# An attention-plus-mixture kernel on one core: TensorE's order chosen while the program is emitted, relu on the freer engine, the first batch loaded in three pieces

## The chip, the cores and the metric

The kernel runs on one core of one Trainium2 chip. The metric is the device time of one execution in microseconds (us), as the median of several runs. All runs told here are of the state that is listed as fast. TensorE's clock is not always granted in full: every record of it in these profiles says either full or half rate (in the kernel before, half at 40.6 to 47.5 us and at 64.5 to 71.4 us, full between them).

The profile names engines in short: PE is TensorE (matrix products), PEld its weight loads, DVE VectorE, ACT ScalarE, POOL GpSimd, SP SyncE. L365 is line 365 of that kernel.

## The reference

```python
# q, k, v: (4 batches, 8 heads, 768 positions, 64);  n_sink = 4, window = 128
scores = q @ k.T / sqrt(64)
keep   = (key < 4) | (0 <= query - key < 128)        # "sink" keys, and a sliding window
x      = softmax(where(keep, scores, -1e9)) @ v      # -> (3072 tokens, 512)
p      = domain_probs / (domain_probs.sum(-1) + 1e-9)  # (3072, 4)
out    = sum over 4 experts e of  p[:, e] * (relu(x @ w1[e]) @ w2[e])   # w1: 512x1024, w2: 1024x512
```

Attention is little work and has long chains (product, exp, mask, product, division, transpose). The mixture is much work and has short ones (product, relu; product, scaled addition). Attention of batch b+1 is therefore mixed into the mixture of batch b. Batch 0 has no earlier mixture to hide in.

## The kernel before

TensorE runs its products in the order of the program, so the order in which the kernel emits them decides what waits for what. The kernel before emits by a fixed pattern. Attention units (batch, head pair, group of 256 queries) go through three product steps with a lag of one unit:

```python
def lagged(units):
    n = len(units)
    for i in range(n + 2):
        if i < n:
            scores(*units[i]); yield          # then exp on ScalarE, mask on VectorE
        if i >= 2:
            turn(*units[i - 2])               # transpose of the scaled values
        if 1 <= i <= n:
            values(*units[i - 1])             # then 1/sum and scaling on VectorE
        yield
```

The mixture pays out attention steps by a counter of TensorE time. In batch 0 there is one step per 500 ns, and later one per 2200 ns. A first-layer part can't start before all attention of its tokens is emitted:

```python
def spent(ns):
    clock["pe"] += ns
    while side and clock["pe"] >= clock["due"]:
        clock["due"] += clock["pace"]
        if next(side[0], "end") == "end": side.pop(0)

def mixture(b, e, part):
    t0, n = PARTS[b][part]                    # batch 0: 3 parts of 256 tokens; later: 2 of 384
    while any((b, hp, t // G) not in turned for ...):
        next(side[0])                         # attention first, whatever it waits for
    for fb in range(NFB):                     # 8 blocks of the hidden layer
        ... 4 matmuls into hp_ (two PSUM banks in turn)
        nc.scalar.activation(out=ht, in_=hp_, func=AF.Relu)
        spent(4 * (n / 2.4 + 3))
        if fb % 2 == 1 and pending:
            pending.pop(0)()                  # second layer: 8 matmuls of 512 columns, DVE adds
    ...
```

The loads, in order of issue (sizes as read, 4 bytes an element): first 256 positions of q and k of batch 0 (1 MB); two blocks of v; w1 of expert 0 (2 MB); w2 of expert 0 (2 MB); the other 512 positions of q and k (2 MB); four blocks of v; w1 and w2 of experts 1 to 3 (12 MB); then q, k and v of batch 1.

The softmax here doesn't subtract the row's maximum and nothing guards it: scores larger than these inputs give would overflow.

## Time and profile before

| | before |
|---|---|
| median time | 447.5 us |
| span of the profile | 445.9 us |
| TensorE busy | 402.4 us |
| ScalarE, VectorE busy | 195.5, 156.3 us |
| end of the last product | 441.8 us |

The page of the kernel before, its parts 1 and 2. Part 2 cuts the span in 40 slices; a digit is the busy share in tenths, and in the row of the clock the granted share.

```profile
PE 402.4 (90%) x2858; PEld 228.5 (51%) x2900; DVE 156.3 (35%) x321; ACT 195.5 (44%) x361; POOL 45.6 (10%) x98
...
PE   2566758999999989999999989999999999999996
...
PEclk9998887999999999999999999999999999999999
DMA  9999996690000115900000110000000110000012
```

TensorE bounds the kernel from about 80 us on. In the first seven slices it is far from full, and DMA is full in the first six of them. A busy TensorE isn't a TensorE at its peak (from 40 to 60 us it is busy for 16.4 us and does 12.9 us of work by the count that follows), so I also counted work. To each product I gave its start-to-start time at full clock, from stretches where nothing waits: 216 ns for 512 columns, 162 for 384, 109 for 256, 56 for a transpose, 31 to 83 for the small attention products. The whole program is 380 us of such work. The rest is lost time. (This trace lacks some products: it has 726 of the 768 of the second layer. I scaled its sum to 380.)

The busy time of each engine in five stretches of the kernel before. The columns are stretch and length, then PE, PEld, DVE, ACT and POOL with numbers of instructions, granted clock, DMA share and GB/s.

```profile
0.00:20.00 20.00, 9.30 (x76) 5.79 (x76) 11.30 (x37) 7.03 (x11) 16.44 (x46) 1.00 1.17 193
20.00:40.00 20.00, 10.64 (x109) 7.52 (x109) 8.45 (x15) 10.58 (x15) 7.29 (x9) 1.00 1.44 199
40.00:60.00 20.00, 16.39 (x156) 10.62 (x158) 9.76 (x26) 8.15 (x15) 3.49 (x4) 0.83 1.21 208
60.00:80.00 20.00, 13.22 (x103) 8.95 (x103) 4.08 (x5) 6.89 (x12) 1.09 (x6) 0.83 0.94 89
80.00:340.00 260.00, 251.50 (x1893) 143.15 (x1921) 99.47 (x208) 126.55 (x236) 17.28 (x34) 1.00 0.22 31
```

The granted clock of 1.00 in the first two rows isn't a reading. The first record of the clock is at 30.4 us, and up to there consecutive transposes start 107 ns apart, against 56 ns from 30.9 us on: half rate.

By the count of work, the four stretches up to 80 us hold 34.9 us of the 380. From there to the last product the rate is 345.1 us of work in 361.8 us, or 95.4%.

What TensorE waited for in the kernel before (total us, times, longest us):

```profile
PE tr L218 <- DVE qo L100: 11.3, 3, 6.6
PE tx L303 <- DVE onat L294: 6.7, 11, 1.2
PE tr L218 <- ACT ko L98: 4.4, 2, 3.3
PE hps L390 <- ACT ht L396: 4.3, 9, 1.0
PE tr L218 <- DVE ko L100: 3.5, 1, 3.5
```

The transposes `tr` wait for q and k that have only just landed: at 22.0 and 24.6 us for the second piece of batch 0, and at 62.1 and 66.1 us for batch 1. The turn `tx` waits for VectorE's scaling, the first layer `hps` for relu.

### The profile page before, as it was taken

The page shows a single profiled execution, that of the slowest core. Times are in us where ns is not written, and L with a number is a line of the kernel's source. Part 1 is how long each engine was busy: PE and PEld are TensorE (multiplying, and loading weights), DVE is VectorE, ACT ScalarE, POOL GpSimd, SP SyncE. Part 2 cuts the span into 40 slices and gives each one's busy share as a digit, 9 for nine tenths or more (in the row PEclk, how much of TensorE's full clock was granted, in tenths as well). Part 3 has the DMA queues.
Part 4 walks back from the last instruction along what each step waited for, and adds up shares of the span by engine and source line. Part 5 has one row for each costly group of instructions (what it writes and reads, how often), then busy time and mean ns, then how long its engine had stood idle before and what let it go on. Part 6 is the DMA issues. An engine that isn't in the chain of part 4 may idle for free.

```text
span 445.9 us, 7024 instructions
## 1 busy us (share of the span) xinstructions
PE 402.4 (90%) x2858; PEld 228.5 (51%) x2900; DVE 156.3 (35%) x321; ACT 195.5 (44%) x361; POOL 45.6 (10%) x98
## 2 busy tenths in 40 slices
PE   2566758999999989999999989999999999999996
PEld 1344436656666655555555554555545555555552
DVE  3825521243444511444443412354442222222222
ACT  3256325545444465544443364454543333333330
POOL 9642100600000006000000010000000000000000
PEclk9998887999999999999999999999999999999999
DMA  9999996690000115900000110000000110000012
GB/s 185 203 193 209 210 195 43 84 129 1 1 2 24 72 49 79 134 2 1 1 1 0 72 71 1 1 1 1 0 1 1 71 72 1 0 1 0 1 47 94
DMA packets 45315, 25.16 MB, mean 56 GB/s; under 512 B 25804, under 2 KB 40140, under 8 KB 45284
## 3 DMA queue, kind: packets, MB, share of 16 engines
q0 software_dynamic: 39552, 17.30, 30.7%
q1 hardware_dynamic: 5732, 7.42, 4.7%
q8 instruction: 22, 0.36, 0.3%
q14 instruction: 9, 0.07, 0.1%
HBM read 35.73 MB, written 6.29 MB: 94 GB/s over the span
## 4 chain that ended last, share of the span: by engine, by line
PE 78%; DMA 12%; ACT 4%; issue 2%; POOL 2%; DVE 1%; ACTq 0%
PE mop L365 36%; PE hps L390 34%; DMA kn<-in_k_dram 8%; DMA vx_72<-in_v_dram 4%; PE sps L250 2%; PE tr L218 2%; ACT ht L396 2%; PE od L287 2%; ACT aT L260 1%; ACT qkT L221 1%; PE tx L303 1%; DVE out_sb L373 1%; PE od L281 1%; POOL vx_72 L109 0%; POOL qn L86 0%
## 5 line engine op out<-in xcount | busy, mean ns | idle before, releaser
L396 ACT ACTIVATE ht<-hps 128x384 bf16<-128x384 f32 (+1 forms) x288 | 128.9, 455 | 171.1 <-PE hps L390 169.2
L365 PEld LDWEIGHTS <-ht 128*128 128x128 bf16 x768 | 74.3, 98 | 79.4 <-issue 3.3
L373 DVE SCALAR_TENSOR_TENSOR out_sb<-mop,scale_t,out_sb 128x512 f32<-128x512 f32 x72 | 54.1, 751 | 140.4 <-PE mop L365 140.4
L260 ACT ACTIVATE aT<-sps 128x1024 bf16<-128x1024 f32 (+1 forms) x46 | 44.0, 957 | 33.8 <-PE sps L250 33.1
L390 PE MATMUL hps<-xT,w_0_88 128*128 128x384 bf16 (+1 forms) x288 | 52.6, 324 | 2.6 <-ACT ht L396 2.4
L390 PE MATMUL hps<-xT,w_2_305 128*128 128x384 bf16 (+1 forms) x288 | 48.8, 308 | 1.0 <-ACT ht L396 0.4
L390 PE MATMUL hps<-xT,w_3_309 128*128 128x384 bf16 (+1 forms) x288 | 48.4, 308 | 1.1 <-ACT ht L396 1.0
L390 PE MATMUL hps<-xT,w_1_301 128*128 128x384 bf16 (+1 forms) x288 | 48.8, 308 | 0.7 <-ACT ht L396 0.5
L365 PE MATMUL mop<-w_0_100,ht 128*128 128x512 bf16 x180 | 45.0, 385 | 0.8 <-issue 0.2
L365 PE MATMUL mop<-w_1_303,ht 128*128 128x512 bf16 x181 | 44.0, 379 | 0.7 <-issue 0.2
L365 PE MATMUL mop<-w_2_307,ht 128*128 128x512 bf16 x181 | 44.0, 379 | 0.7 <-issue 0.2
L365 PE MATMUL mop<-w_3_311,ht 128*128 128x512 bf16 x184 | 44.1, 379 | 0.4
L371 DVE TENSOR_SCALAR out_sb<-mop,scale_t 128x512 f32<-128x512 f32 x24 | 18.0, 751 | 59.5 <-PE mop L365 57.8
L390 PEld LDWEIGHTS <-w_0_88 128*128 128x128 bf16 x288 | 28.1, 103 | 20.1 <-issue 6.9
L261 DVE TENSOR_TENSOR aT<-aT,mask_93 128x1024 bf16<-128x1024 bf16 x32 | 22.1, 692 | 40.7 <-ACT aT L260 40.7
L390 PEld LDWEIGHTS <-w_3_309 128*128 128x128 bf16 x288 | 27.1, 98 | 17.7 <-issue 3.7
L390 PEld LDWEIGHTS <-w_1_301 128*128 128x128 bf16 x288 | 26.6, 97 | 17.0 <-issue 4.3
L390 PEld LDWEIGHTS <-w_2_305 128*128 128x128 bf16 x288 | 26.4, 97 | 16.7 <-issue 4.5
L221 ACT COPY qkT<-tr 128x1536 bf16<-128x1536 bf16 (+2 forms) x16 | 20.5, 1278 | 23.4 <-PE tr L218 23.4
L218 PE MATMUL tr<-ident,qo 128*128 128x128 bf16 x96 | 9.9, 238 | 13.2 <-DVE qo L100 11.3
L294 DVE TENSOR_TENSOR onat<-od,R 128x256 bf16<-128x256 f32 x48 | 20.4, 425 | 1.7
L303 PE MATMUL tx<-ident,onat 128*128 128x128 bf16 x96 | 14.0, 230 | 6.8 <-DVE onat L294 6.7
(73 smaller groups left out, 226.5 us busy)
## 6 DMA issues: line engine op xcount, KB each, us to landing
out_dram<-out_sb SPq DMA_DIRECT2D x24, 256.0 KB
qn<-in_q_dram POOLq DMA_DIRECT2D x3, 768.0 KB, 8.0
kn<-in_k_dram POOLq DMA_DIRECT2D x3, 768.0 KB, 10.9
vx_72<-in_v_dram POOLq DMA_DIRECT2D x12, 128.0 KB, 10.9
vx_73<-in_v_dram POOLq DMA_DIRECT2D x12, 128.0 KB, 12.1
w_0_88<-in_moe_w_dram POOLq DMA_DIRECT2D x1, 1024.0 KB, 10.3
w_0_100<-in_moe_w_dram POOLq DMA_DIRECT2D x1, 1024.0 KB, 14.2
w_1_301<-in_moe_w_dram POOLq DMA_DIRECT2D x1, 1024.0 KB, 16.1
```

Source lines behind the costliest of these rows:

```text
L218: nc.tensor.transpose(tr[:, i, t], nat[b, piece, name][:, t, 2 * hp:2 * hp + 2, :], ident,)
L221: (nc.vector.tensor_copy if b == 0 and hp % 2 else nc.scalar.copy)(out=qkT[b, hp][:, :, s0:s0 + T * P].rearrange("c i (p t) -> c i p t", t=T),
L250: nc.tensor.matmul(sps[ph][:, c:c + nq * P], lhsT=T[pr, 1, kb * P:(kb + 1) * P], rhs=T[pr, 0, qb * P:(qb + nq) * P], start=True, stop=True,)
L260: nc.scalar.activation(out=a, in_=both[:, :, 0:w], func=AF.Exp, scale=scale)
L261: nc.vector.tensor_mul(a, a, m[:, None, :].to_broadcast([P, 2, w]))
L294: nc.vector.tensor_mul(o, od[:, :, :, 0:D], R.to_broadcast([P, 2, 2, D]))
L303: nc.tensor.transpose(tx[:, qi], o[:, qi], ident)
L365: nc.tensor.matmul(op, lhsT=hts[fb][:, off:off + P], rhs=w2_sb[e][:, fb, :], start=(fb == 0), stop=(fb == NFB - 1),)
L371: nc.vector.tensor_scalar(out=dst, in0=op, scalar1=sc, scalar2=None, op0=ALU.mult)
L373: nc.vector.scalar_tensor_tensor(out=dst, in0=op, scalar=sc, in1=dst, op0=ALU.mult, op1=ALU.add,)
L390: nc.tensor.matmul(hp_, lhsT=w1_sb[e][:, db, fb * P:(fb + 1) * P], rhs=xT[b, db][:, t0:t0 + n], start=(db == 0), stop=(db == NDB - 1),)
L396: nc.scalar.activation(out=ht, in_=hp_, func=AF.Relu)
```

## The change

Its intent is to keep TensorE in ready work. There are four parts:

1. A rough clock of all engines runs while the program is emitted, and a chooser takes the step that is ready. The whole control flow of the mixture and of attention becomes two classes with a list of options.
2. Relu and the copies out of PSUM go to whichever of ScalarE and VectorE is free sooner by that clock.
3. Batch 0 is loaded in three pieces instead of two, piece 1 ahead of w2, and expert 3's weights behind batch 1.
4. TensorE multiplies zeros until data lands, to release its clock (in the kernel before, the first record of the full clock is at 30.4 us). Banks and the sink copies were moved a little as well.

The core of the diff (cut at "..."):

```diff
-    PIECES = {b: [(0, 2), (G, 4)] if b == 0 else [(0, NQB)] for b in range(B)}
+    PIECES = {b: [(0, 2), (G, 2), (2 * G, 2)] if b == 0 else [(0, NQB)] for b in range(B)}
+    t = {"pe": 0.0, "act": 0.0, "dve": 0.0}
+    def pe(cols, *deps):
+        t["pe"] = max(t["pe"], *deps) + cols / 2.4 + 2
+        return t["pe"] + 170
+    def act(cols, *deps):
+        t["act"] = max(t["act"], *deps) + 190 + cols / 1.2
+        return t["act"] + 60
+    def dve(cols, *deps, rate=0.96):
+        t["dve"] = max(t["dve"], *deps) + 130 + cols / rate
+        return t["dve"] + 60
+    def lands(key, nbytes):
+        dma["at"] += nbytes / 350.0
+        landed[key] = dma["at"] + 1500
...
-    load_w2(0)
-    load_qk(0, 1)
-    load_v(0, (2, 3, 4, 5))
+    load_qk(0, 1)
+    load_v(0, (2, 3))
+    load_w2(0)
...
+            engine, at = sooner(n, end)
+            if engine == "act":
+                nc.scalar.activation(out=ht, in_=hp_, func=AF.Relu)
+            else:
+                nc.vector.tensor_scalar(out=ht, in0=hp_, scalar1=0.0, scalar2=None, op0=ALU.max)
...
-    regroup(0, 0)
+    warm, _ = two_banks()
+    idle_products(warm[0], 10)                 # ten 512-column products of zeros
+    regroup_first()
     for hp in range(NHP):
         transposes(0, 0, hp, tag="ho"[hp // 2])
+        idle_products(warm[0], 1, 256)
...
     values(0, 1, 0)
-    turn(0, 0, 0)
-    values(0, 2, 0)
-    turn(0, 1, 0)
-    values(0, 3, 0)
+    regroup(0, 1)
+    values(0, 2, 0, tag="h")
+    turn(0, 0, 0, tag="o")
+    turn(0, 1, 0, tag="o")
+    values(0, 3, 0, tag="h")
...
-    for e in range(1, E):
+    load_qk(0, 2)
+    load_v(0, (4, 5))
+    for e in (1, 2):
         load_w1(e)
         load_w2(e)
...
+    while mix.more() or att.more():
+        now = t["pe"]
...
+        due = ahead == 0 or att.steps * share <= (mix.done - upto) * att.total
+        opts = []
+        if att.more():
+            opts = [(max(r, now), 0 if due else 3, "att", step) for r, step in att.options()]
+        f, s2 = mix.first_ready(), mix.second_ready()
+        opts.append((max(f, now), 2, "first", None))
+        opts.append((max(s2, now), 1 if mix.since >= 2 else 2.5, "second", None))
+        r, _, kind, step = min(opts, key=lambda o: (o[0] > now + 40, o[0] if o[0] > now + 40 else 0, o[1]))
...
```

## The prediction

> **What bounds the kernel now.** TensorE: the page gives it 402.4 of 445.9 us busy, and the chain of waits is 78% TensorE, 12% DMA. Summing start-to-start times at full clock from the timeline (512-column product 216 ns, 384: 162, 256: 109, transpose 56, small attention products 31 to 83), the mixture needs about 332 us and attention 48: 380 us. The other 66 us (work done per 20 us window, against that sum):
> - Up to 80 us only about 35 us of work is done; 45 lost. The first transpose starts at 6.6 us; transposes wait 2.7 and 3.3 us for the second piece of q and k (landing at 22.0 and 24.6 us, behind 2 MB of w2); second-layer work starts only at 47 us, as attention goes first and each turn waits about 0.8 us for VectorE; batch 1's q and k land at 62 and 66 us, behind all weights: waits of 2.0 and 3.5 us. And the clock: 128-column transposes start 107 ns apart at 8 us, 56 ns later; the profile records half clock at 40.7–47.5 and 64.6–71.4 us. [...] half rate up to about 30 us, with idle gaps of 0.5 to 3 us.
> - From 80 to 442 us it works at about 95.5%; 98.6% in the last 100 us, mixture alone (10.53 us for 10.38). In between, waits for relu and regrouped q, k.
> - The end: 4 us after the last product.
>
> **What the change does.**
> 1. Warm-up: ten 512-column zero products (about 4.3 us at half rate) before data lands. Off the chain; should release the clock by 6 to 8 us.
> 2. First loads halved by heads; second piece 1 MB of q, k instead of 2, ahead of w2. At the landings' 350 to 390 bytes/ns it should land near 16 us.
> 3. One expert's weights (4 MB) fewer ahead of batch 1: its q, k land near 55 to 60 us.
> 4. Order chosen while emitting: mixture fills attention's waits; from about 19 us TensorE should rarely wait.
> 5. Relu: 66 of 288 go to VectorE (instruction order), some copies to ScalarE. About 30 us moves from ScalarE (195) to VectorE (156). Neither bounds; worth a few us at most.
>
> **Sum.** By 19 us about 4 us of work is done (15 lost); 19 to 62 us: about 39. At 80 us I expect about 60 done against 35: 25 gained. The remaining 320 at 97% instead of 95.5%: 331 us, about 6 more gained. 80 + 331 + 4 end + 1.5 outside the span: **about 415 us** (estimate from these durations), range 406 to 426. Chances: faster by over 2% 0.96, within 2% 0.03, slower 0.01.
>
> **Signs.** TensorE over 95% busy in every slice after 20 us; no half clock after 8 us; second-layer products by 27 us; no wait over 1 us on batch 1's regrouped q, k; ScalarE about 175 us, VectorE 175 to 185; the last 80 us and the end unchanged.
>
> **What would make it wrong.** TensorE runs a fixed order: where the rough clock believes data too early (VectorE's 512-column eviction took 751 ns, the clock has 663) it stalls while other work is ready: 420 to 430. Zero products that don't release the clock: 5 us worse. If nearly all stalls go: 405 to 408.

No term of the sum is cut with it; its terms are 80 + 331 + 4 + 1.5 = 416.5 us, given there as about 415. That zeros "should release the clock by 6 to 8 us", and the "5 us worse" without it, stand as estimates; measured were a full clock from 5.6 us in one profile and from 10.6 us in another, and 419.9 us without any zeros.

## The result, and the profile after

The changed kernel takes 420.1 us (median of 4 runs, 419.86 to 420.7) against 447.5 us. The ratio is 0.939 with a 95% interval of 0.9374 to 0.9406, so it is faster by 6.1%. A ratio here and below is the mean time of one kernel's fast runs over that of the other's of the same rounds, so it is not quite the ratio of the medians that are quoted.

The page after, parts 1 and 2:

```profile
PE 398.6 (95%) x2874; PEld 229.3 (55%) x2918; DVE 176.0 (42%) x349; ACT 188.7 (45%) x336; POOL 50.1 (12%) x94
...
PE   6598899999999999999999999999999999999996
...
PEclk9599899999999999999999999999999999999999
DMA  9999999292011129200002100000001100000012
```

The same five stretches after:

```profile
0.00:20.00 20.00, 12.13 (x84) 6.43 (x85) 10.06 (x30) 8.33 (x14) 16.08 (x47) 0.72 1.31 181
20.00:40.00 20.00, 18.52 (x191) 12.66 (x190) 12.87 (x31) 11.67 (x21) 10.02 (x13) 0.93 1.39 201
40.00:60.00 20.00, 17.73 (x145) 11.18 (x147) 11.81 (x27) 5.93 (x10) 5.10 (x6) 0.91 1.50 195
60.00:80.00 20.00, 19.56 (x163) 13.56 (x164) 10.77 (x21) 9.93 (x9) 1.28 (x5) 1.00 0.70 113
80.00:340.00 260.00, 257.05 (x1919) 147.57 (x1948) 113.25 (x219) 126.78 (x229) 17.61 (x26) 1.00 0.23 37
```

And what TensorE waited for after, longest total first (the waits of the first zero products and transposes, up to 9 us, and a 1.4 us row of issue are left out):

```profile
PE tx L427 <- DVE onat L412: 3.0, 3, 1.9
PE od L402 <- DVE aT L363: 2.4, 3, 1.3
...
PE tr L299 <- ACT qkT L135: 1.3, 3, 0.6
```

The waits for regrouped q and k after landing are gone. Waits for relu are no longer listed either.

The same account of work, from a second profile of the changed kernel that lacks no product (that of its second run, told near the end; zero products are not counted as work):

| | work done by 80 us | of it up to 20, 20–40, 40–60, 60–80 | rate from 80 us to the last product |
|---|---|---|---|
| before | 34.9 us | 4.1, 7.3, 12.9, 10.6 | 95.4% |
| after | 52.0 us | 3.5, 14.8, 14.7, 19.0 | 98.0% |

The 17.1 us more by 80 us would have taken the kernel before 17.9 us at its later rate. The remaining 328 us take 334.5 us instead of 343.9, another 9.4 us. Together that is 27.3 us, which is what the end of the last product moved (441.8 to 414.5 us). Two thirds of the gain lie in the first 80 us.

### The profile page after: what moved, and what is told of

The parts are those of the page before. It is cut to its first block, busy times and chain, and to the rows that moved or that the text cites. A ratio compares the mean times of both kernels' runs of the same rounds, so it can differ in the third digit from the quotient of the medians.

```text
span 417.9 us, 7002 instructions
## 1 busy us (share of the span) xinstructions
PE 398.6 (95%) x2874; PEld 229.3 (55%) x2918; DVE 176.0 (42%) x349; ACT 188.7 (45%) x336; POOL 50.1 (12%) x94
## 4 chain that ended last, share of the span: by engine, by line
PE 91%; DMA 3%; ACT 2%; POOL 1%; DVE 1%; issue 1%; ACTq 0%
PE hps L547 41%; PE mop L582 39%; PE sps L351 3%; DMA kn<-in_k_dram 3%; PE tr L299 3%; PE od L402 2%; PE tx L427 1%; ACT aT L362 1%; PE od L395 1%; POOL vx L177 0%; ACT qkT L135 0%; DVE ht L558 0%; PE sps L330 0%; DVE aT L363 0%; ACT ko L135 0%
## 5 line engine op out<-in xcount | busy, mean ns | idle before, releaser
L547 PE MATMUL hps<-xT,w 128*128 128x384 bf16 (+1 forms) x1152 | 195.6, 310 | 0.5
L582 PE MATMUL mop<-w,ht 128*128 128x512 bf16 x724 | 174.5, 379 | 3.3 <-issue 1.4
L556 ACT ACTIVATE ht<-hps 128x384 bf16<-128x384 f32 (+1 forms) x222 | 103.0, 470 | 149.3 <-PE hps L547 148.3
L547 PEld LDWEIGHTS <-w 128*128 128x128 bf16 x1152 | 108.2, 98 | 62.3 <-issue 8.4
L363 DVE TENSOR_TENSOR aT<-aT,mask 128x1024 bf16<-128x1024 bf16 (+1 forms) x46 | 31.2, 678 | 50.9 <-ACT aT L362 50.7
L558 DVE TENSOR_SCALAR ht<-hps 128x256 bf16<-128x256 f32 (+1 forms) x66 | 29.8, 451 | 18.9 <-PE hps L547 16.9
L590 DVE TENSOR_SCALAR out_sb<-mop,scale_t 128x512 f32<-128x512 f32 x24 | 18.0, 750 | 34.9 <-PE mop L582 34.8
L135 ACT COPY qkT<-tr 128x1536 bf16<-128x1536 bf16 (+1 forms) x20 | 21.9, 1098 | 16.5 <-PE tr L299 16.5
L135 ACT COPY xT<-tx 128x256 bf16<-128x256 bf16 x32 | 11.9, 374 | 26.6 <-PE tx L427 26.0
L402 PE MATMUL od<-vx,aT 128*128 128x65 bf16 x352 | 20.9, 197 | 2.4 <-DVE aT L363 2.4
L177 POOL DMA_DIRECT2D vx<-in_v_dram x24 | 21.3, 915 | 9.8 <-DMA w<-in_moe_w_dram 9.8
L351 PE MATMUL sps<-qkT 64*128 64x128 bf16 (+1 forms) x256 | 18.4, 246 | 0.5
L395 PE MATMUL od<-vsd,sinkA 128*128 128x130 bf16 x64 | 12.9, 220 | 0.0
```

The source lines that it names most:

```text
L135: (nc.scalar.copy if engine == "act" else nc.vector.tensor_copy)(out=out, in_=in_)
L177: nc.gpsimd.dma_start(out=vx[b % 2][:, tb, :, 0:D], in_=v[b, :, tb * P:(tb + 1) * P, :].rearrange("h p d -> p h d"),)
L351: nc.tensor.matmul(sps[ph][:, c:c + nq * P], lhsT=T[pr, 1, kb * P:(kb + 1) * P], rhs=T[pr, 0, qb * P:(qb + nq) * P], start=True, stop=True,)
L363: nc.vector.tensor_mul(a, a, m[:, None, :].to_broadcast([P, 2, w]))
L402: nc.tensor.matmul(od[:, qi, ph], lhsT=a[:, ph, c:c + P], rhs=vx[b % 2][:, kb, 2 * hp + ph, 0:DX], start=(g == 0 and i == 0), stop=(i == l ...
L547: nc.tensor.matmul(hp_, lhsT=w1_sb[e][:, db, fb * P:(fb + 1) * P], rhs=xT[b, db][:, t0:t0 + n], start=(db == 0), stop=(db == NDB - 1),)
```

## The experiments

The theory (A) was: about half of the gain is the order, about half the loads, the place of relu is worth little, and the zeros nothing. The rivals were: the loads alone (B), the order alone (C), relu on the freer engine (D), the warm clock (E). Four of the runs each undo one part of the changed kernel: its order, its loads, its place of relu, its zeros. (The banks and sink copies that were moved as well were undone in no run.) I add the account of work where it tells something.

### The order of before, in the changed kernel

The chooser's loop is replaced by the pattern of before; loads, zeros, relu rule and copies stay, and the rough clock still picks the engine of a copy.

```diff
-    while mix.more() or att.more():
-        ...chooser...
+    for (b, e, part, fb) in list(mix.first):
+        ...loads and side.append(attention(b + 1)) at the points of before...
+        if fb == 0:
+            while any((b, hp, x // G) not in turned ...): next(side[0])
+        waiting = len(mix.second)
+        mix.emit_first(); spent(4 * (n / 2.4 + 3))
+        if fb % 2 == 1 and waiting:
+            mix.emit_second(); spent(1730)
```

> The changed kernel with its loads, zero products, relu rule and copies, but TensorE's order set as in the kernel before (a fixed lag of one attention unit, one attention step per 0.5 us of mixture in batch 0 and per 2.2 us later, one second-layer group after every second first-layer group). Theory A (the order is about half of the gain, the loads the other half): 430 to 438 us, with the early waits of transposes for VectorE's scaled values back. Rival B (the loads are the gain, the order adds nothing): 424 us or less. Rival C (the order is all of it): 443 us or more.

Measured: 437.3 us, ratio 0.9759 (0.9745 to 0.9774). That is 0.037 of the time before above the changed kernel, 16.5 us. Work by 80 us is 42.2 us and the rate after it 96.0%, so the order acts in both stages. What TensorE waited for in this run:

```profile
PE tx L427 <- DVE onat L412: 8.5, 11, 2.0
PE tr L299 <- ACT qkT L135: 4.1, 6, 0.9
PE tr L299 <- ACT ko L135: 3.2, 1, 3.2
PE hps L547 <- ACT ht L556: 1.8, 6, 0.4
```

The eleven waits of the turn for VectorE are back, and transposes of batch 1 are emitted before k has landed.

### The loads of before, in the changed kernel

```diff
-    PIECES = ... [(0, 2), (G, 2), (2 * G, 2)] if b == 0
+    PIECES = ... [(0, 2), (G, 4)] if b == 0
-    load_qk(0, 1); load_v(0, (2, 3)); load_w2(0)
+    load_w2(0); load_qk(0, 1); load_v(0, (2, 3, 4, 5))
-    for e in (1, 2):                  # and expert 3 behind batch 1
+    for e in (1, 2, 3):
```

The attention list of batch 0 starts with regrouping and transposing that second piece. The first piece still comes in halves by heads, as in the changed kernel.

> The changed kernel with its chooser, but the loads as before: the rest of batch 0's q and k in one piece of 2 MB behind w2 of expert 0, all weights ahead of batch 1. Theory A: 427 to 434 us, the transposes of batch 0's second piece wait until about 27 us, and those of batch 1 until about 67 us. Rival B (loads are the gain): 440 us or more. Rival C (order is all of it): 423 us or less.

Measured: 429.8 us, ratio 0.9588 (0.9572 to 0.9604), or 8.9 us above the changed kernel. Work by 80 us is 43.4 us and the rate after it 97.7%. So the loads act in the first 80 us nearly alone. The first transposes of the second piece started at 29.0 us. The detail about batch 1 was wrong: its q and k landed at 63.2 and 67.1 us, but its transposes started at 79.9 us with waits of 0.3 us or less. The chooser had put other work first, so nothing stood and waited as it did in the kernel before:

```profile
29.03 0.40 PE L299 MATMUL tr<-ident,qo 128*128 128x128 bf16 x4 [1.45 <-DVE qo L135]
...
79.87 0.51 PE L299 MATMUL tr<-ident,qo 128*128 128x128 bf16 x6 [0.27 <-DVE qo L135]
```

This run undoes two changes of the loads at once. By the count of work it does 8.4 us between 20 and 40 us, where the changed kernel does 14.8; that is 6.4 of the 8.6 us that it lacks by 80 us. So most of the loss lies where batch 0's second piece comes late. What moving expert 3's weights is worth isn't isolated: in the changed kernel batch 1's k landed at 57.2 us and its transposes began only at 68.5 us.

### Every relu on ScalarE, in the same order

```diff
             engine, at = sooner(n, end)
-            if engine == "act":
+            if True:
                 nc.scalar.activation(out=ht, in_=hp_, func=AF.Relu)
```

> The changed kernel in the same order, but every relu on ScalarE. Theory A (neither engine bounds, relu's place is worth little): 420.5 to 424 us, a few waits of first-layer products for ScalarE come back. Rival D (the freer engine for relu is a main part of the gain): 428 us or more.

Measured: 424.25 us, ratio 0.9467 (0.9445 to 0.9488), or 3.4 us above the changed kernel. It is just beyond the upper end of A's range and far from D's. Five listed waits of the first layer for relu return:

```profile
PE hps L547 <- ACT ht L556: 3.4, 5, 1.0
```

In this run the rough clock believed some relus to be on VectorE. A later run told it the truth, and the order changed with it:

```diff
-            engine, at = sooner(n, end)
+            engine, at = "act", act(n, end)
```

> Every relu on ScalarE, and the rough clock is told so (in the earlier run with all relus on ScalarE it was not, and the order was the changed kernel's). If part of that run's loss of some 3.4 us came from a clock that was wrong about it: 421 to 423 us. If all of it is ScalarE's load: 423.5 to 425 us again.

Measured: 424.05 us, ratio 0.9467 (0.9453 to 0.9481), the same. So the loss is the same with a rough clock that knows of it: it is ScalarE's load that costs 3.4 us, and not a wrong clock. It does so in the stage with attention: after the last product of attention all three kernels (the changed one and these two) work at 99.6%. ScalarE is busy 212 us of 421 in the first of these runs; it costs time although it is far from full.

### No products of zeros

```diff
-    idle_products(warm[0], 10)
...
-        idle_products(warm[0], 1, 256)
```

> The changed kernel without any product on zeros. Theory A (the clock fell back to half at 9.0 us by the record, so the zeros bought full rate for some 3 us of little work): 419.5 to 421.5 us, no full-clock record before about 22 us. Rival E (the warm-up is worth what it was meant for): 424 us or more.

Measured: 419.9 us, ratio 0.9369 (0.9354 to 0.9383), which is no different from the changed kernel (the intervals overlap) and within A's range. The zeros did release the clock in the profile that came with the result. The transposes of the changed kernel first, start and duration in us:

```profile
6.67 0.28 PE L299 MATMUL tr<-ident,qf 128*128 128x128 bf16 x2 [0.97 <-DVE qf L135]
6.79 0.28 PE L299 MATMUL tr<-ident,kf 128*128 128x128 bf16 x2
...
9.19 0.42 PE L279 MATMUL sps<-zeros 128*128 128x256 bf16 x1
9.40 0.42 PE L299 MATMUL tr<-ident,qf 128*128 128x128 bf16 x2
```

Without zeros:

```profile
6.67 0.40 PE L299 MATMUL tr<-ident,qf 128*128 128x128 bf16 x2 [6.67 <-DVE qf L135]
6.86 0.42 PE L299 MATMUL tr<-ident,kf 128*128 128x128 bf16 x2
```

The first transposes ran at twice the rate with zeros (from 6.8 us on they start 56 ns apart, without zeros 107), and the first record of the full clock is at 5.6 us, without zeros only at 23.3 us. But the next ones wait for data anyway, and by the record the clock is back at half from 8.98 to 22.63 us. In the second profile of the changed kernel the first record of the full clock is only at 10.6 us, so even that little isn't had in every run. The prediction's "5 us worse" without a release was wrong: without any zeros nothing is lost.

### Four edits towards what the prediction had counted on

The changed kernel had done 52 us of work by 80 us, where I had expected 60. Two stretches are poor in its profile: up to 21.6 us (half clock from 9.0 us, waits before the first mixture), and 46.5 to 53.4 us. The products of the changed kernel at the second:

```profile
47.37 0.22 PE L395 MATMUL od<-vsd,sinkA 128*128 128x130 bf16 x1
48.92 0.29 PE L402 MATMUL od<-vx,aT 128*128 128x65 bf16 x4 [1.33 <-DVE aT L363]
...
49.48 0.28 PE L427 MATMUL tx<-ident,onat 128*128 128x128 bf16 x2
50.22 0.37 PE L427 MATMUL tx<-ident,onat 128*128 128x128 bf16 x2 [0.46 <-ACT xT L135]
50.39 2.98 PE L547 MATMUL hps<-xT,w 128*128 128x256 bf16 x13
```

The last attention units of batch 0 run one after another with nothing between. The mixture's first layer is a strict list, and its next entry (expert 0, last part) needs just these units. Expert 1's weights had landed at 34.4 and 39.4 us. By the records TensorE is idle for 1.9 us between 47.4 and 50.4 us (the text below says about 2.5). From 49.94 to 53.35 us the clock is at half, so 14 of the next 36 first-layer products start at half rate.

The first edit puts one block of expert 1 (its first part: 8 hidden blocks, 32 products) ahead of that entry. The last added line leaves the order of the other two blocks of expert 1 as it was:

```diff
+            block = lambda e, part: [(0, e, part, fb) for fb in range(NFB)]
+            n = 4 * NFB
+            self.first[0:n] = block(0, 0) + block(0, 1) + block(1, 0) + block(0, 2)
+            self.first[n:6 * NFB] = block(1, 1) + block(1, 2)
```

> The changed kernel with one edit: in batch 0 the first-layer products of expert 1's first parts come ahead of expert 0's last part, so that TensorE has ready work while the last attention units of batch 0 finish (47 to 50 us in the changed kernel's trace, where it idles about 2.5 us and the clock falls to half for 3.4 us). Theory A (the strict order of the first layer leaves this hole): 416 to 418 us, no wait of values for VectorE over 0.5 us near 48 us and no half clock near 50 us. Rival (other waits close in behind): 419.5 to 421 us.

Measured: 416.9 us, ratio 0.9312 (0.9297 to 0.9328), or 3.5 us less than the changed kernel, as A had it. The half clock near 50 us is gone, work by 80 us is 55.0 us, and first-layer products stand in the hole:

```profile
50.57 0.28 PE L427 MATMUL tx<-ident,onat 128*128 128x128 bf16 x2
51.14 0.60 PE L551 MATMUL hps<-xT,w 128*128 128x256 bf16 x4 [0.30 <-ACT ht L560]
51.58 0.22 PE L395 MATMUL od<-vsd,sinkA 128*128 128x130 bf16 x1
```

The second edit moves `regroup(0, 1)` behind `values(0, 3, 0)` in the program:

> The changed kernel with the copies that regroup piece 1 of q and k emitted after, not before, the values of the third and fourth head pair, so that VectorE's queue isn't held by a copy that waits for q's landing at 16.6 us. Theory A (the wait of 1.9 us at 16.1 us goes, but the chain runs through k's landing at 18.1 us and its copy, so the time stays): 419.3 to 420.3 us. Rival F (this in-order wait costs what it shows): 418 us.

Measured: 420.9 us, ratio 0.9401 (0.9383 to 0.9419), no different from the changed kernel and just above A's range. In the changed kernel VectorE's copy of q waited for its landing until 16.64 us, and the two reciprocals behind it started only at 17.32 and 18.06 us, though their products were done by 14.1 and 16.1 us. With the edit the turns end at 17 us instead of 19, but the transposes of k then wait for k itself:

```profile
16.82 0.40 PE L427 MATMUL tx<-ident,onat 128*128 128x128 bf16 x2 [0.52 <-DVE onat L412]
17.57 0.39 PE L299 MATMUL tr<-ident,qo 128*128 128x128 bf16 x2 [0.36 <-DVE qo L135]
19.56 0.40 PE L299 MATMUL tr<-ident,ko 128*128 128x128 bf16 x2 [1.59 <-ACT ko L135]
```

They start at 19.56 us; in the changed kernel it was 19.62 us. A wait that was removed off the critical path came back as another one.

The third edit puts zeros (transposes and products) into TensorE's gaps between 7.8 and 19.4 us, into banks that the real ones then start anew. The trace has 71 of them against 14 in the changed kernel, so 57 more, not 45:

```diff
+        for i in range(fill):
+            nc.tensor.transpose(tx[:, i % 2], zeros[:, 0:P], ident)     # in turn(); likewise in
+                                                                        # values() and transposes()
-        idle_products(warm[0], 1, 256)
+        idle_products(warm[0], 5 if hp == 1 else 1, 512 if hp == 1 else 256)
```

> The changed kernel with about 45 more products or transposes of zeros put into TensorE's idle gaps between 7.8 and 19.4 us (into banks that the real ones then start anew), to see what the half clock from 9.0 to 22.6 us costs. Theory A (some 4 us of work runs at half rate there, part of it hidden by waits for other engines): the record shows no half clock between 9 and 22 us, and 417.5 to 419 us. Rival G (all of that is hidden behind landings): 420 us. If the gaps' zeros don't hold the clock, or delay the real work: 420 to 421 us.

Measured: 419.7 us, ratio 0.9377 (0.936 to 0.9395), no different from the changed kernel within its interval; that is above A's range, and near rival G's figure. The clock did hold: full from 10.1 us to the end, without a record of half rate between. So the half rate from 9 to 22 us, which looks costly in the record, cost little: the mean ratios differ by 0.0013 (0.6 us), and the ends of the two intervals, 0.9406 and 0.936, allow about 2 us at most. The filling isn't quite free either. In the profiled run five of the zero products still ran at half rate and held the next transposes back until 9.86 us, though only the last k was still to come. So a gain of a microsecond or two from a full clock stays possible; it isn't shown.

All three together:

> The three edits together. Theory A: the holes are separate and add up, 413.5 to 416.5 us. Rival: they are one delay seen three times, no better than the best single one.

Measured: 416.9 us, ratio 0.9312 (0.9285 to 0.9339). That is just outside A's range, and no better than the first edit alone. Its runs scatter more (415.56 to 418.16 us) than the others'. The profiled run was the fastest (415.56 us), so its 57.1 us of work by 80 us is not typical. What makes this kernel scatter stays open. The kernel with expert 1 early is therefore the one to keep: it beats both kernels by a clear margin.

### How good must the rough clock be?

The prediction named a rough clock that is wrong as the main danger. Two runs make it wrong: the durations of ScalarE and VectorE are halved or doubled in `act`, `dve` and `sooner`. The changed kernel was run beside them: 420.3 us, ratio 0.9384.

```diff
-        t["act"] = max(t["act"], *deps) + 190 + cols / 1.2
+        t["act"] = max(t["act"], *deps) + 0.5 * (190 + cols / 1.2)     # 2.0 in the other
```

> The changed kernel unaltered, as the measure for the others of this call: ratio to the kernel before 0.937 to 0.941, about 420 us.

> The changed kernel, with the rough clock's durations of ScalarE and VectorE halved (so it believes results ready too early) and nothing else touched. Theory A (the chooser's gain comes from knowing about when a result is ready; a fixed program order then stalls where it was told too little): 423 to 430 us, with 5 to 10 us of waits of TensorE for the other two in place of some 10 in all. Rival H (any order that mixes attention into the mixture does as well): 419 to 421.5 us.

Measured with half: 433.8 us, ratio 0.9685 (0.9669 to 0.9701), 13.5 us worse than the changed kernel beside it, above A's range. Work by 80 us is 51.7 us, as in the changed kernel, but the rate after it falls from 98.0 to 94.8%, below the kernel of before. TensorE's waits in this run:

```profile
PE tx L427 <- DVE onat L412: 5.4, 9, 1.7
PE od L402 <- DVE aT L363: 4.1, 9, 1.0
PE hps L547 <- DVE ht L558: 1.8, 5, 0.5
```

Listed waits rise by some 6 us in all. The remaining loss isn't in the list, and only the account of work shows it. The likely reason, argued and not shown, is overlap: a 512-column product lasts 379 ns on the changed kernel's page but starts 216 ns after the one before it, so a short wait leaves no idle time between the two records.

> The same with these durations doubled (results believed late). Theory A: attention is put off rather than stalled on, which costs little while there is mixture to do: 419.5 to 424 us, with fewer waits than the changed kernel after 60 us. Rival H: 419 to 421.5 us.

Measured with double: 430.7 us, ratio 0.9614 (0.96 to 0.9628), 10.3 us worse and far above A's range. My reason was wrong. Here the rate after 80 us is nearly kept (97.4%), and work by 80 us falls to 43.6 us. With doubled durations the rough clock ran ahead of real time, while its landing times stayed. By its own formula k of batch 1 lands at about 62 us (19.5 MiB through 350 bytes per ns, plus 4 us). TensorE reached the transposes at 54.85 us of real time; k landed at 57.5 us, and ScalarE's copy of it ended at 60.3 us:

```profile
54.85 0.84 PE L299 MATMUL tr<-ident,qo 128*128 128x128 bf16 x6
60.34 0.82 PE L299 MATMUL tr<-ident,ko 128*128 128x128 bf16 x6 [4.64 <-ACT ko L135]
```

The clock was at half already before these transposes (eight first-layer products from 53.15 us took 1.91 us, against 1.04 at full rate), and by the record up to 66 us. So a clock that is pessimistic about two engines became optimistic about DMA. This is read from the trace; no run corrects the landing times alone. Both runs also change what `sooner` picks, so a part of their loss can be the engine of relus and copies and not the order; having every relu on ScalarE cost 3.4 us.

## Why the prediction was right, and where it was off

The time was predicted as 415 us with 406 to 426; it is 420.1 us. The direction and the mechanism hold: TensorE's lost time shrank, two thirds of it before 80 us. By parts, each undone by itself: order 16.5 us, loads 8.9 us, relu 3.4 us, zeros nothing. They sum to 28.8 us against a gain of 27.3 us (0.061 of 447.5), so they hardly overlap. The prediction's own terms add up to 416.5 us, not 415.

- **"At 80 us I expect about 60 done against 35: 25 gained."** This term was too large: 52 done, 17 gained. One cause is shown: the hole at 47 to 50 us with the half clock after it, from the strict list of first-layer parts. Filling it gave 3.0 us of work by 80 us. The rest isn't isolated. The first mixture product started at 21.6 us, not 19, as q and k of piece 1 landed at 16.6 and 18.1 us and each needs a copy. From 20 to 60 us, the hole included, TensorE's work rate is about 74% (29.5 of 40 us); what else holds it there was not tested.
- **"The remaining 320 at 97% instead of 95.5%."** This term was too small: 328 us at 98.0%, a gain of 9.4 us and not 6. The two errors have opposite signs, which is why the total came close: that part is luck.
- **"No half clock after 8 us."** Wrong: half from 9.0 to 22.6 us and from 49.9 to 53.4 us. The first cost nothing that could be measured (the run with a full clock throughout was no different within its interval), the second went with the hole.
- **The zeros "should release the clock by 6 to 8 us".** They did by the record at 5.6 us in one profile, and at 10.6 us in the other; it wasn't worth any time.
- **Landings.** The "350 to 390 bytes/ns" are an estimate: in the kernel before, 7.5 MiB as read had landed by 24.6 us and 23.5 MiB by 66.1 us (in order of issue), which is 320 and 373 bytes per ns from the start of the span, and 404 between the two. Piece 1 near 16 us: 16.6 and 18.1 us. Batch 1 at 55 to 60 us: 53.3 and 57.2 us. Its transposes no longer waited.
- **"Second-layer products by 27 us."** They began at 29.0 us.
- **"ScalarE about 175 us, VectorE 175 to 185."** VectorE 176.0 us. ScalarE 188.7 us: relu left, but the chooser gave it 32 of the 48 copies of the turned values (11.9 us), which I had put too low.
- **"TensorE over 95% busy in every slice after 20 us."** Not between 30 and 50 us (90% and 80% in two stretches of 10 us).
- **Relu "worth a few us at most".** 3.4 us.
- **"The last 80 us and the end unchanged."** Right: mixture alone, and 3.9 us after the last product (before: 4.1).
- **The rough clock as the danger.** Factors of two cost 10 to 13 us. Its small errors (663 ns for a measured 751) were not tested by themselves.

## What to carry to other kernels

Where an engine runs a fixed order, choosing that order by a model of when results are ready can be worth more than moving work between engines that aren't full (here 16.5 us against 3.4), but the model must be about right on all engines and, as the trace with doubled durations suggests, on DMA relative to them. Count work at full rate per stretch of time, not busy time or waits: the first shows where time is lost and what a change gave back, and the listed waits missed about half of the loss in the run with halved durations. Before you remove a wait or a half clock that stands out in a profile, ask what the next product would wait for; two of three such repairs here changed nothing measurable, and the one that gave TensorE other ready work paid.
